# Chunk attention followed by a GELU MLP: plain V loads, tiles of the array by chunk parity, and a new order of transfers and products in the last five tiles

## The chip, the cores and the metric

The kernel runs on one NeuronCore of a Trainium2 chip. The metric is the device time of one execution in microseconds (us); lower is better. The core has five engines that run beside each other and meet at semaphores: TensorE (in the profile PE for matmuls, PEld for the loading of their weights), VectorE (DVE), ScalarE (ACT), GpSimd (POOL) and SyncE (SP), which issues nearly all DMAs of this kernel.

## The reference

```python
# q, k, v: 8 batches x 8 heads x 576 positions x 64, cut into 9 chunks of 64 positions
scores = matmul(q_c, k_c.T) / sqrt(64)               # each chunk attends to itself alone
attn = exp(scores - max) ; attn /= sum(attn) + 1e-9
x = matmul(attn, v_c)       # then heads side by side: 4608 tokens x 512
h = x @ w_in                # 512 x 2048
g = 0.5 * h * (1 + erf(h / sqrt(2)))
y = g @ w_out               # 2048 x 512, float32 out
```

## The kernel before

**Tiles.** The 4608 tokens are nine tiles of 512. Tiles 0 to 7 are the first eight chunks of each batch; tile 8 (`B`) gathers the ninth chunk of all batches. A tile's attention runs while the MLP of the tile before it runs: the outer loop has a step t for each MLP tile, and within step t stands the attention of tile n = t+1, the transposes of tile t+2, and loads of tiles t+2 and t+3. `FIRSTX` = 4 is the first tile whose attention takes the row form (`rows_av`, `rows_x`), which the change alters, and `FIRST7` = 3 is the first step whose second product has seven multiplications.

**The MLP of a step.** Both products are done with seven half-size products in the place of eight (Strassen's scheme in Winograd's form), so sums of blocks are needed as operands. `mm1_groups` makes h: 28 products of four matmuls, in the written order `FOUR` (steps 3 to 7). There `1a` is the first product of column group a, and `c1a`, `c2a`, `c3a` are copies of a bank by ACT, ACT and DVE. `6a` needs the third sum that `x_sums` (L602) makes of x. `c3c` (L706) writes into a buffer of the pool `ypool`. `h1` to `h3` call `h_sums` (L556, L557), two sums of h. Then `mm2_seven` makes y with seven products of 16 matmuls of 256 columns (L727, L736) in three PSUM banks X, Y and Z of a ring of three (`ps_mm`). Its fourth and fifth products need `h_third` (L561) and `h_fourth` (L565), sums of h by DVE. Before the change the order is: X; `rows_av`; Y; X again; Y again; Z = s3*T3 with its two output halves; Y += s4*w; Z += h*T4. `also(i)` marks the points where other work is inserted, as the lists `e2` say.

**The y buffers.** `ypool` has two buffers. A step from 3 to 7 takes three tiles of it in this order: one at `c3c`, y[0], y[1]. So `c3c` of the next step always takes the buffer of this step's y[0], and has to wait until both stores of y[0] have read it.

**Attention of a tile.** `quad_S` (L232) makes scores in four PSUM banks, 64 matmuls of 64 by 64 with the array cut into four tiles (row half r, column half o); ACT takes the exponential. V lies on 128 partitions as two chunks of 64 keys. `load_v_rows` (L120) puts the odd heads one chunk further than the even ones, so it takes nine DMAs for a tile, and 16 for tile 8. With that layout `rows_av` (L328) gives each of the four tiles of the array one matmul in each round of four: (0,0), (1,0), (1,1), (0,1). `rows_x` divides by the sums (L346, L348) and issues two DMA transposes (L340), the second when all is divided; they give the x of the next MLP. q and k are loaded (L108, L102; tile 8: L111, L106), cast by POOL (L154) and transposed by DMA (`flips_of`, L187). V is cast by POOL too (L206).

**Order.** The program is written out by hand (`manual_schedule`): each engine takes its own instructions in the order of the program, SP too. A DMA that waits on SP, or waits for its turn in the queue, holds back what is behind it. In step t before the change, SP has at the begin of `mm1_groups` (`ahead`): the transposes of q and k of tile t+2, and V of tile t+2 (steps 4, 5; in step 3 the q of tile 6); at `also(1)` the transposes of x, then q of tile t+3; then stores of y (L827) with k of tile t+3 at `also(4)`.

**The end.** Step 8 ends with `last_seven`: the last two products work on y[1], L811 adds its right half, L814 its left half, and `store_rows` (L821) stores a block of whole rows on two queues (SP and ACT).

Of the kernel before, what the change touches and what calls it, by code (L numbers as in the profile page):

```python
# [11 lines left out]
def kernel(  # L12
# [9 lines left out]
    nc = tc.nc  # L22
# [69 lines left out]
    def load_qk(t, nm, h0=0, h1=H):  # L92

        st = tiles[t]
        src = q if nm == "q" else k
        if nm + "f" not in st:
            st[nm + "f"] = stage_tile()[:].rearrange("p (h j d) -> p h j d", h=H, j=J)
            st[nm] = ld.tile([P, G, J, 2, D], bf16, tag=nm, name=f"{nm}_nat", bufs=1)
        raw = st[nm + "f"]
        if nm == "k" and t < B and t not in ORDERED:  # L100
            for n in range(CT // 2):
                nc.sync.dma_start(raw[:, :, n], src[t, :, P * n:P * (n + 1), :].rearrange("h key d -> key h d"))  # L102
        elif nm == "k" and t == B:
            for b in range(B):
                c, n = b % 2, b // 2
                nc.sync.dma_start(raw[CH * c:CH * (c + 1), :, n], src[b, :, MT:S, :].rearrange("h key d -> key h d"))  # L106
        elif t < B:
            nc.sync.dma_start(raw[:, h0:h1], src[t, h0:h1, 0:MT, :].rearrange("h (p j) d -> p h j d", j=J))  # L108
        else:
            for h in range(h0, h1):  # L110
                nc.sync.dma_start(raw[:, h], src[:, h, MT:S, :].rearrange("b (p j) d -> b p j d", j=J))  # L111

    def load_v_rows(t, parity=range(2)):

        if "vf" not in tiles[t]:
            tiles[t]["vf"] = stage_tile()[:].rearrange("p (h n d) -> p h n d", h=H, d=D)
        raw = tiles[t]["vf"]

        def go(to, rows):
            nc.sync.dma_start(to, rows.rearrange("h key d -> key h d"))  # L120
        last = CT // 2 - 1
        if t < B and 0 in parity:
            for n in range(CT // 2):
                go(raw[:, 0::2, n], v[t, 0::2, P * n:P * (n + 1), :])
        if t < B and 1 in parity:
            for n in range(last):
                go(raw[:, 1::2, n], v[t, 1::2, CH + P * n:CH + P * (n + 1), :])
            go(raw[0:CH, 1::2, last], v[t, 1::2, MT - CH:MT, :])
            go(raw[CH:P, 1::2, last], v[t, 1::2, 0:CH, :])
        if t == B:  # L130
            for b in range(B):
                for r in parity:
                    c, n = place(r, b)
                    go(raw[CH * c:CH * (c + 1), r::2, n], v[b, r::2, MT:S, :])

    def load_v_plain(t):
        tiles[t]["vf"] = stage_tile()[:].rearrange("p (h n d) -> p h n d", h=H, d=D)
# [84 lines left out]
    def quad_S(t, pairs=(0, 1)):  # L222

        st = tiles[t]
        if pairs[0] == 0:
            st["s_ps"] = four_banks("s_ps")
        s_ps = st["s_ps"]
        for g2, u, g, n, r, c, o, rs, os in quadrants():
            if g2 not in pairs:
                continue  # L230
            i = 2 * n + c
            nc.tensor.matmul(s_ps[g2][c][os, u, :].rearrange("p (j c) -> p j c", j=J),  # L232
                             st["kt"][rs, g * J + n, CH * c:CH * (c + 1)],
                             st["qt"][rs, g * J:(g + 1) * J, i * PC:(i + 1) * PC],
                             start=True, stop=True, tile_position=(CH * r, CH * o))
# [80 lines left out]
    def rows_av(t, last):  # L316
# [5 lines left out]
        for b in range(G * CT // 2):  # L322
            for c in range(2):
                for r in range(2):
                    bank, i = 2 * (b // NX) + r, b % NX
                    g, n, o = b // (CT // 2), b % (CT // 2), c ^ r
                    os, cs = slice(CH * o, CH * (o + 1)), slice(CH * c, CH * (c + 1))
                    nc.tensor.matmul(st["av"][bank][cs, i, :],  # L328
                                     st["pT", 2 * (g // 2) + c][os, CT // 2 * (g % 2) + n, :],
                                     st["v"][os, 2 * g + r, place(r, 2 * n + c)[1], :],  # L330
                                     start=True, stop=True, tile_position=(CH * o, CH * c))

    def rows_x(t):

# [404 lines left out]
    def halves(bank):  # L739
        return [bank[:, 0], bank[:, 1]]  # L740

    def mm2_seven(t, at={}):

        def also(i):
            for u in at.get(i, ()):
                u()
# [32 lines left out]
        TT(y[1][:, :, NH:], Z[:], s5[:], op=add)  # L779
        store(t, 1, 1, y)  # L780
        also(3)
        product(halves(Y), s[4], w[:, 1, :, 1], False)
        AC(y[0][:, :, NH:], Y[:])
        store(t, 0, 1, y)
        also(4)
        product(halves(Z), h[:, 1, :, 1], T[4], False)
        TT(y[1][:, :, :NH], Z[:], s2[:], op=add)
        store(t, 1, 0, y)
        also(5)

    def last_seven(t, h, w, s, T, banks, sums, y):
# [19 lines left out]
        product(Zs, s[3], T[3], True, lambda m: TT(y[1][:, m, NH:], Zs[m], s5[:, m], op=add))  # L811

        def row_block(m):
            TT(y[1][:, m, :NH], Zs[m], s2[:, m], op=add)  # L814
            store_rows(t, 1, m, y)
        product(Zs, h[:, 1, :, 1], T[4], False, row_block)

    def store_rows(t, th, m, y):
        for c in range(P // CH):
            m0 = ((th * (TH // P) + m) * (P // CH) + c) * S + MT  # L820
            (nc.sync if c == 0 else nc.scalar).dma_start(out[m0:m0 + CH, :], y[th][c * CH:(c + 1) * CH, m, :])  # L821

    def store(t, th, nh, y):

# [110 lines left out]
    with tc.manual_schedule():  # L935
# [126 lines left out]
        for t in range(1, NT):  # L1062
# [15 lines left out]
            elif t == 2:  # L1078
# [4 lines left out]
                def behind_k():  # L1083
# [1 line left out]
                    nc.gpsimd.tensor_copy(tiles[4]["q"][:, 0, 0, 0, 0:1], tiles[3]["kt"][:, G * J - 1, 0:1])  # L1085
                    pool_cast_qk(4)
                    flips_of(4)
                    load_v_rows(4)
                    load_qk(5, "q")
                    cast_v_rows(4, PO)  # L1090
                e1[f"i{G - 1}"] = [behind_k]
                e2 = one_tile(3, {8: [lambda: load_qk(5, "k")], 12: [lambda: quad_S(4, (0,))], 13: [lambda: quad_S(4, (1,)), lambda: act_table(Act.Gelu)]})
            elif n < NT:
                def ahead(t=t):
                    first = (0,) if t == B - 3 else ()
                    if FIRST7 < t < B - 2:
# [3 lines left out]
                    if FIRST7 < t < B - 2:  # L1100
                        load_v_rows(t + 2, [r for r in range(2) if r not in first])
                    if t == FIRST7:
                        load_ahead(t, "q")
                    if t == B - 1:
                        load_v_rows(B, (1,))
                        cast_v_rows(B, PO)
# [5 lines left out]
                def behind(t=t):  # L1112
                    load_ahead(t, "k")
# [12 lines left out]
                e2 = {1: [lambda: rows_av(n, tiles[n - 1]["Z"]), lambda: rows_x(n)], 2: [], 3: [], 4: [behind, lambda: x_sums(n)]}  # L1126
                if t == FIRST7:
                    e2[2] += [late_v]
                if FIRST7 < t < B - 2:
                    e2[1] += [lambda t=t: cast_v_rows(t + 2, PO)]  # L1130
                if t == B - 2:
                    e2[1] += [lambda: load_v_rows(B, (0,))]
                if t + 3 < NT:
                    if t > FIRST7:
                        e2[1] += [lambda t=t: load_ahead(t, "q")]
                    if t + 3 < B:
                        e2[1] += [lambda t=t: pool_cast_q(t + 3)]
                if n + 1 < NT:
                    e2[1] = [lambda: act_table(Act.Exp)] + e2[1]
                    e2[2 if t == FIRST7 else (2, 0)] = e2[2] + [lambda: quad_S(n + 1), lambda: act_table(Act.Gelu)]  # L1140
            phase(t, e1, e2, between=last_rows if t == 1 else {})
# [1 line left out]
_INS = ['q', 'k', 'v', 'moe_w_in', 'moe_w_out']  # L1143
# [26 lines left out]
```

## Time and profile before

| | |
|---|---|
| time, median of 3 runs | 272.56 us (271.09 to 273.3) |
| profiled execution, first to last instruction | 273.1 us; no other time of it is given, and it lies within the range of the three runs |
| PE busy | 262.1 us, 96% |
| DVE, ACT, POOL busy | 73%, 68%, 29% |
| granted clock of TensorE | 0.997 on average |
| DMA | 56.60 MB, mean 207 GB/s; the queue of SP takes 79.2% of the 16 engines' span |

How to read it: a busy time of PE is from the start of a matmul to its modelled end, and matmuls overlap, so that starts tell more than ends. In the lists of instructions in order of time the columns are: start in us from the span's start, duration of the merged group, engine (a q behind it: its sequencer, which issues DMAs), line, operation, output<-inputs, shapes, count, and in brackets the idle time before it with what ended it.

### The profile page before, as it was taken

Reading aid. Unit: us, or ns where it says so; the run is one execution under the profiler, and the core shown is the slowest. Engines: PE = TensorE matmul, PEld = TensorE weight load, DVE = VectorE, ACT = ScalarE, POOL = GpSimd, SP = SyncE. Lnnn points to the kernel's source line nnn. Section 1 sums busy time; section 2 is a strip of 40 time slices with the busy share of each in tenths; the row PEclk is TensorE's granted clock in tenths of the full one; section 3 lists DMA queues with packets and bytes.
Section 4 is the critical chain, followed back from the end, with each engine's and each line's share of the span. In section 5 each row is a group of like instructions: output and inputs, shape, how many; then the busy total and the mean of one; then the engine's idle time right before and its main releaser. Section 6 shows DMA issues by size and latency. Waiting matters only on the chain. (4 is left out here: it accounts for less than half of the span.)

```text
span 273.1 us, 7571 instructions
## 1 busy us (share of the span) xinstructions
PE 262.1 (96%) x3080; PEld 194.2 (71%) x3080; DVE 198.1 (73%) x363; ACT 186.9 (68%) x363; POOL 79.3 (29%) x127
## 2 busy tenths in 40 slices
PE   8989999999999999999989999989998999999993
PEld 3454453486458544888878888878887888888782
DVE  2663787959898697599479937995699559946851
ACT  3557756788767967886679669956995699338600
POOL 2734667351370240342333043311062011000000
PEclk9999999999999999999999999999999999999998
DMA  6999999997979799898989989998895571340005
GB/s 201 261 344 406 395 396 232 265 278 162 337 206 223 198 204 207 242 258 149 275 218 252 193 167 307 238 188 144 252 228 113 107 217 32 74 159 2 1 4 154
DMA packets 128564, 56.60 MB, mean 207 GB/s; under 512 B 103952, under 2 KB 123408, under 8 KB 128528
## 3 DMA queue, kind: packets, MB, share of 16 engines
q1 hardware_dynamic: 128208, 55.59, 79.2%
q8 instruction: 24, 0.39, 0.6%
q10 hardware_dynamic: 320, 0.52, 0.5%
q14 instruction: 12, 0.10, 0.1%
HBM read 36.70 MB, written 9.44 MB: 169 GB/s over the span
## 5 line engine op out<-in xcount | busy, mean ns | idle before, releaser
L658 PEld LDWEIGHTS <-w_in_s 128*128 128x128 bf16 x464 | 45.2, 98 | 7.4 <-DVE x_t L602 1.1
L658 PEld LDWEIGHTS <-w_in_sb 128*128 128x128 bf16 x348 | 33.9, 98 | 7.2 <-issue 1.0
L206 POOL CAST v_nat<-arrival 128x1024 bf16<-128x1024 f32 x14 | 16.3, 1164 | 61.8 <-DMA arrival<-in_v_dram 54.8
L727 PEld LDWEIGHTS <-h_s 128*128 128x128 bf16 x304 | 29.3, 98 | 5.6 <-DVE h_s L561 2.1
L836 PE MATMUL y_ps<-w_out_sb,h 128*128 128x512 bf16 x144 | 33.0, 380 | 0.0
L658 PE MATMUL h_Y<-x_t,w_in_s 128*128 128x256 bf16 x232 | 32.0, 272 | 1.0 <-DVE x_t L602 0.8
L658 PE MATMUL h_X<-x,w_in_sb 128*128 128x256 bf16 x232 | 32.6, 273 | 0.0
L727 PEld LDWEIGHTS <-h 128*128 128x128 bf16 x288 | 28.2, 98 | 3.5
L154 POOL CAST k_nat<-arrival 128x512 bf16<-128x512 f32 x34 | 22.3, 692 | 25.3 <-DMA arrival<-in_k_dram 20.8
L154 POOL CAST q_nat<-arrival 128x512 bf16<-128x512 f32 x33 | 19.6, 633 | 26.1 <-DMA arrival<-in_q_dram 25.9
L727 PE MATMUL y_ps<-w_t,h_s 128*128 128x256 bf16 x208 | 25.1, 273 | 1.6 <-DVE h_s L561 1.6
L836 PEld LDWEIGHTS <-h 128*128 128x128 bf16 x144 | 13.4, 98 | 15.0 <-issue 0.2
L693 ACT COPY h_Y<-h_X 128x512 f32<-128x512 f32 x29 | 16.4, 582 | 9.7 <-PE h_X L658 9.5
L727 PE MATMUL y_ps<-w_out_sb,h 128*128 128x256 bf16 x192 | 22.9, 273 | 0.0
L933 ACT ACT_TABLE_LOAD x16 | 20.5, 1283 | 1.0 <-PEq L1154 0.7
L665 ACT ACTIVATE h<-h_Y 128x512 bf16<-128x512 f32 x29 | 17.0, 593 | 1.8 <-PE h_Y L658 1.3
L665 ACT ACTIVATE h<-h_X 128x512 bf16<-128x512 f32 x29 | 17.2, 598 | 1.4 <-PE h_X L658 0.8
L239 ACT ACTIVATE pT<-s_ps 128x512 bf16<-128x512 f32 x28 | 14.5, 601 | 4.3 <-PE s_ps L232 4.2
L658 PE MATMUL h_Z<-x_t,w_in_s 128*128 128x256 bf16 x116 | 17.4, 273 | 0.0
L658 PE MATMUL h_Z<-x_t,w_in_sb 128*128 128x256 bf16 x116 | 16.9, 272 | 0.4 <-DVE h_d L709 0.4
L658 PE MATMUL h_Y<-x,w_in_s 128*128 128x256 bf16 x116 | 16.9, 273 | 0.0
L706 DVE COPY h_a<-h_Y 128x512 f32<-128x512 f32 x8 | 5.5, 691 | 14.8 <-PE h_Y L658 14.8
(148 smaller groups left out, 490.9 us busy)
## 6 DMA issues: line engine op xcount, KB each, us to landing
out_dram<-y_sb SPq DMA_DIRECT2D x32, 256.0 KB
arrival<-in_q_dram SPq DMA_DIRECT2D x7, 1024.0 KB
arrival<-in_k_dram SPq DMA_DIRECT2D x24, 256.0 KB
arrival<-in_v_dram SPq DMA_DIRECT2D x42, 128.0 KB
arrival<-in_moe_w_out_dram SPq DMA_DIRECT2D x4, 1024.0 KB
arrival<-in_v_dram SPq DMA_DIRECT2D x8, 256.0 KB
arrival<-in_moe_w_in_dram SPq DMA_DIRECT2D x4, 512.0 KB
arrival<-in_moe_w_in_dram SPq DMA_DIRECT2D x2, 1024.0 KB
```

What stands on the lines that cost most here:

```text
L154: copy(st[nm][:, g].rearrange("p j r d -> p r j d"), st[nm + "f"][:, 2 * g:2 * g + 2])
L206: copy(st["v"][:, r::2, :, :D], st["vf"][:, r::2])
L239: nc.scalar.activation(pT[:].rearrange("p u (c j) -> p u c j", j=J), s_ps[g2][c][:].rearrange("p u (j c) -> p u c j", j=J), Act.Exp, scale ...
L658: nc.tensor.matmul(banks[g + name][:, i], lhs[:, kk, i], rhs[:, kk], start=fresh and i == kk == 0, stop=(kk == 1), skip_group_check=True)
L665: nc.scalar.activation(h[:, j:j + 2, m], src[:], Act.Gelu)
L693: AC(banks[g + "Y"][:], banks[g + "X"][:])
L706: (AC if i == 0 else DV)(sums[g, i][:], banks[g + "Y"][:])
L727: nc.tensor.matmul(out[m], lhs[:, f, m * P:(m + 1) * P], rhs[:, f, :], start=fresh and f == 0 and (m == 0 or len(out) == 3), stop=(f == FH ...
L836: nc.tensor.matmul(y_ps[:], st["h"][:, f, ms * P:(ms + 1) * P], w_out_sb[:, f, :], start=(f == 0), stop=(f == FF - 1))
L933: nc.scalar.activation(act_scratch[:], rest[:, 0:1], func)
```

## The change

Five edits, all from tile 4 on (or step 3 on):

1. **V in four plain transfers.** `load_v_plain` brings V of tiles 4 to 7 in four DMAs of 256 KB with all heads alike (tile 8: eight DMAs). `place` is plain for these tiles.
2. **Scores and AV by chunk parity.** In `quad_S` the scores of chunk parity c go to the partitions of column half c, and the bank is chosen by r. `rows_av` then uses the tiles (0,0), (0,0), (1,1), (1,1) in each round of four: two tiles of the array, each twice in a row, where there were four.
3. **Order of the transfers.** V of tile t+2 and q of tile t+3 leave the begin of the step and `also(1)`. q and k of tile t+3 are issued at `also(2)`, behind the transposes of x. V of tile t+2 is issued at `also(4)` in steps 3 and 4, and at `also(2)` ahead of q and k in steps 5 and 6. V is cast at the begin of the next step (tiles 5, 6) or right behind its load (tiles 7, 8).
4. **Ninth q.** Its eight DMAs name the position within the chunk first and the batch second, (p b) where it was (b p). The scores of tile 8 read it with a step of eight elements.
5. **Late sums of h later, and the stores.** `mm2_seven` makes Z = h*T4 first, adds it to s2 on DVE, then W = s3*T3 in a fourth turn of the ring, which DVE adds twice into y[1]; y[1] is stored by one DMA of 512 KB. The product with s4, and with it the last store of y[0], is now last. In `last_seven` each half of the columns of y[1] is stored as soon as it is there.

```diff
-                nc.sync.dma_start(raw[:, h], src[:, h, MT:S, :].rearrange("b (p j) d -> b p j d", j=J))
+                nc.sync.dma_start(raw[:, h], src[:, h, MT:S, :].rearrange("b (p j) d -> p b (j d)", j=J))
...
-    def place(r, i):
+    def place(r, i, t=0):
+        if t >= FIRSTX:
+            return i % 2, i // 2
...
-            nc.tensor.matmul(s_ps[g2][c][os, u, :].rearrange("p (j c) -> p j c", j=J),
+            if t >= FIRSTX:
+                o, os = c, slice(CH * c, CH * (c + 1))
+            nc.tensor.matmul(s_ps[g2][r if t >= FIRSTX else c][os, u, :].rearrange("p (j c) -> p j c", j=J),
                              st["kt"][rs, g * J + n, CH * c:CH * (c + 1)],
+                             st["qt"][rs, g * J:(g + 1) * J, i:P:CT] if t == B else
...
-                                     st["pT", 2 * (g // 2) + c][os, CT // 2 * (g % 2) + n, :],
-                                     st["v"][os, 2 * g + r, place(r, 2 * n + c)[1], :],
-                                     start=True, stop=True, tile_position=(CH * o, CH * c))
+                                     st["pT", 2 * (g // 2) + r][cs, CT // 2 * (g % 2) + n, :],
+                                     st["v"][cs, 2 * g + r, n, :],
+                                     start=True, stop=True, tile_position=(CH * c, CH * c))
...
-        product(halves(Z), s[3], T[3], True, lambda m: also((2, m)))
-        TT(y[1][:, :, NH:], Z[:], s5[:], op=add)
-        store(t, 1, 1, y)
+        product(halves(Z), h[:, 1, :, 1], T[4], True, lambda m: also((2, m)))
+        TT(s2[:], Z[:], s2[:], op=add)
         also(3)
+        W = bank_mm()
+        product(halves(W), s[3], T[3], True)
+        TT(y[1][:, :, NH:], W[:], s5[:], op=add)
+        TT(y[1][:, :, :NH], W[:], s2[:], op=add)
+        store_whole(t, 1, y)
+        also(4)
         product(halves(Y), s[4], w[:, 1, :, 1], False)
         AC(y[0][:, :, NH:], Y[:])
         store(t, 0, 1, y)
-        also(4)
-        product(halves(Z), h[:, 1, :, 1], T[4], False)
-        TT(y[1][:, :, :NH], Z[:], s2[:], op=add)
-        store(t, 1, 0, y)
...
+        def row_block(m, nh):
+            cols = slice(nh * NH, (nh + 1) * NH)
+            TT(y[1][:, m, cols], Zs[m], (s2, s5)[nh][:, m], op=add)
+            store_rows(t, 1, m, y, cols)
+        product(Zs, s[3], T[3], True, lambda m: row_block(m, 1))
+        product(Zs, h[:, 1, :, 1], T[4], False, lambda m: row_block(m, 0))
...
-                    load_v_rows(4)
+                    load_v_plain(4)
...
                 def ahead(t=t):
-                    first = (0,) if t == B - 3 else ()
-                    if FIRST7 < t < B - 2:
-                        load_v_rows(t + 2, first)
                     if t + 2 < NT:
                         flips_of(t + 2)
...
+                    if t in (FIRST7 + 1, FIRST7 + 2):
+                        cast_v_rows(t + 1, PO)
+
+                def qk(t=t):
+                    if t + 3 < NT:
                         load_ahead(t, "q")
+                        if t + 3 < B:
+                            pool_cast_q(t + 3)
+                        load_ahead(t, "k")
                 def late_v(t=t):
-                    load_v_rows(t + 2)
-                    cast_v_rows(t + 2, PO)
+                    if t + 2 < NT:
+                        load_v_plain(t + 2)
+                    if t >= FIRST7 + 2 and t + 2 < NT:
+                        cast_v_rows(t + 2, PO)
...
+                e2[2 if t > FIRST7 + 1 else 4].append(late_v)
+                e2[2].append(qk)
```

More of the change, by code (lines that the diff above doesn't have):

```diff
@@ L129, in load_v_rows, with load_v_plain @@
             go(raw[CH:P, 1::2, last], v[t, 1::2, 0:CH, :])
+    def load_v_plain(t):
+        tiles[t]["vf"] = stage_tile()[:].rearrange("p (h n d) -> p h n d", h=H, d=D)
         if t == B:
             for b in range(B):
[L132 to L137, printed above, removed]
+                c, n = b % 2, b // 2
+                nc.sync.dma_start(tiles[t]["vf"][CH * c:CH * (c + 1), :, n], v[b, :, MT:S, :].rearrange("h key d -> key h d"))
+            return
         for n in range(CT // 2):
@@ L325, in rows_av @@
                     bank, i = 2 * (b // NX) + r, b % NX
[L326 to L327 removed]
+                    g, n = b // (CT // 2), b % (CT // 2)
+                    cs = slice(CH * c, CH * (c + 1))
                     nc.tensor.matmul(st["av"][bank][cs, i, :],
[L329 to L331 removed]
+                                     st["pT", 2 * (g // 2) + r][cs, CT // 2 * (g % 2) + n, :],
+                                     st["v"][cs, 2 * g + r, n, :],
+                                     start=True, stop=True, tile_position=(CH * c, CH * c))
     def rows_x(t):
@@ L810, in last_seven, with store_rows, store_whole @@
             store_rows(t, 0, m, y)
[L811 to L818, printed above, removed]
+        def row_block(m, nh):
[4 more added lines that the diff above has]
+        product(Zs, h[:, 1, :, 1], T[4], False, lambda m: row_block(m, 0))
+    def store_rows(t, th, m, y, cols=slice(0, d_model)):
         for c in range(P // CH):
             m0 = ((th * (TH // P) + m) * (P // CH) + c) * S + MT
-            (nc.sync if c == 0 else nc.scalar).dma_start(out[m0:m0 + CH, :], y[th][c * CH:(c + 1) * CH, m, :])
+            (nc.sync if c == 0 else nc.scalar).dma_start(out[m0:m0 + CH, cols], y[th][c * CH:(c + 1) * CH, m, cols])
+    def store_whole(t, th, y):
+        m0 = t * S + th * TH
+        nc.sync.dma_start(out[m0:m0 + TH, :].rearrange("(m p) n -> p m n", p=P), y[th][:])
     def store(t, th, nh, y):
@@ L1125 @@
                     pool_cast_q(t + 2)
[L1126 to L1137, printed above, removed]
+                e2 = {1: [lambda: rows_av(n, tiles[n - 1]["Z"]), lambda: rows_x(n)], 2: [], 3: [], 4: [lambda: x_sums(n)]}
+                e2[2 if t > FIRST7 + 1 else 4].append(late_v)
+                e2[2].append(qk)
                 if n + 1 < NT:
                     e2[1] = [lambda: act_table(Act.Exp)] + e2[1]
-                    e2[2 if t == FIRST7 else (2, 0)] = e2[2] + [lambda: quad_S(n + 1), lambda: act_table(Act.Gelu)]
+                    e2.setdefault(2 if t == FIRST7 else (2, 0), []).extend([lambda: quad_S(n + 1), lambda: act_table(Act.Gelu)])
             phase(t, e1, e2, between=last_rows if t == 1 else {})
```

8 lines of the change are left out of this document (removed).

## The prediction

> **What bounds the kernel now.** I read the page first, then the table of windows cut at the steps, then PE in order of time wherever a step was longer than its matmuls.
>
> ```profile
> span 273.1 us, 7571 instructions
> PE 262.1 (96%) x3080; PEld 194.2 (71%) x3080; DVE 198.1 (73%) x363; ACT 186.9 (68%) x363; POOL 79.3 (29%) x127
> ...
> 135.95:163.22 27.27, 26.41 (x355) 23.00 (x353) 19.83 (x39) 20.63 (x37) 7.63 (x11) 1.00 0.96 206
> 163.22:190.30 27.08, 26.39 (x355) 23.01 (x353) 21.42 (x42) 20.63 (x37) 6.98 (x11) 1.00 1.02 220
> ...
> 165.00:170.00 5.00, 5.00 (x48) 4.41 (x46) 3.29 (x6) 4.60 (x9) 2.17 (x4) 1.00 1.07 329
> ```
>
> The window rows give length, busy time of PE, PEld, DVE, ACT and POOL, clock, DMA share and GB/s; the first two are steps 4 and 5. PE bounds the kernel, at full clock. The DMA engines are almost as full (0.96, 1.02), so what stands early in their queue delays what stands late. All that PE can gain in the middle of the kernel is its few stalls:
>
> ```profile
> 121.20 0.60 PE L658 MATMUL h_Z<-x_t,w_in_sb 128*128 128x256 bf16 x4 [0.36 <-DVE h_d L709]
> ...
> 135.95 1.47 PE L658 MATMUL h_X<-x,w_in_sb 128*128 128x256 bf16 x12
> 138.27 0.61 PE L658 MATMUL h_Y<-x_t,w_in_s 128*128 128x256 bf16 x4 [0.84 <-DVE x_t L602]
> ...
> 173.32 0.60 PE L658 MATMUL h_Y<-x,w_in_s 128*128 128x256 bf16 x4
> 173.76 0.60 PE L658 MATMUL h_Z<-x_t,w_in_sb 128*128 128x256 bf16 x4
> ...
> 181.79 1.80 PE L727 MATMUL y_ps<-w_t,h_s 128*128 128x256 bf16 x15
> 184.25 1.05 PE L727 MATMUL y_ps<-w_t,h_s 128*128 128x256 bf16 x8 [0.67 <-DVE h_s L561]
> ...
> 209.24 1.47 PE L727 MATMUL y_ps<-w_t,h_s 128*128 128x256 bf16 x12
> 211.63 1.05 PE L727 MATMUL y_ps<-w_t,h_s 128*128 128x256 bf16 x8 [0.91 <-DVE h_s L561]
> ```
>
> Four matmuls of 256 columns take 0.437 us from start to start (173.32 to 173.76), so 0.109 each. Counted from starts, the stalls are 1.01 us at 138.27 (2.32 less 12 x 0.109), 0.82 at 184.25 (2.46 less 15 x 0.109) and 1.08 at 211.63; at 121.20 I use the 0.36 of the row.
>
> **The change part by part.** E is the end of a step.
>
> *AV on two tiles of the array.*
>
> ```profile
> 151.17 0.65 PE L328 MATMUL av_ps<-v_nat,pT 64*64 64x65 bf16 x56
> ...
> 151.72 0.21 PE L328 MATMUL y_ps<-v_nat,pT 64*64 64x65 bf16 x1
> 151.95 1.91 PE L736 MATMUL y_ps<-w_t,h_s 128*128 128x256 bf16 x16
> ...
> 158.16 0.74 PE L232 MATMUL s_ps<-q_t,k_t 64*64 64x64 bf16 x64
> ...
> L328 PEld LDWEIGHTS <-pT 64*64 64x64 bf16 x320 | 3.3, 106 | 1.1 <-issue 0.8 <-DVE h_s L557 0.2
> ```
>
> Today 64 matmuls start within 0.55 us (151.17 to 151.72): 16 rounds of four at 0.034 us, in which each tile has one matmul. 65 columns at 0.109/256 need 0.028, so a round is about one streaming time of a tile, and the weights of the next matmul hide behind it. With two tiles, each twice in a row, a round takes two such times: 16 x 0.034 more and a few ns of issue in each, +0.6 us a tile, +3.0 for tiles 4 to 8. Lower end: 32 matmuls of 0.028 are 0.89, so +0.34 each, 1.7 in all. Upper end: weights of a tile that is busy are not hidden, 0.106 for each of two matmuls in 16 rounds, 3.4 us, +2.8 each. I take 3.0, because today's round shows a tile receiving new weights every 0.034 us.
>
> *Scores.* Each round still uses all four tiles once, and neighbours of the kind (0,0), (1,0) stand in today's AV: 0. Tile 8 reads q with a step of eight elements, which no row shows. Between nothing and a doubling of 0.74 (the row at 158.16) I take +0.3. The Trainium skill (SBUF — State Buffer, Door 1: The DMA port swizzle) says that SBUF wants two hits in each 16-byte line for full bandwidth; eight bf16 elements are just one line, so by it every column would pay. No run here shows that yet; the sum would stay within the +0.74 of my upper end.
>
> *Late sums.*
>
> ```profile
> 182.98 1.22 DVE L561 TENSOR_TENSOR h_s<-h 128x2048 bf16<-128x2048 bf16 x1
> 187.05 0.69 DVE L779 TENSOR_TENSOR y_sb<-y_ps,y 128x512 f32<-128x512 f32 x1 [1.72 <-PE y_ps L727]
> 189.15 0.76 DVE L602 TENSOR_TENSOR x_t<-x 128x512 bf16<-128x512 bf16 x2 [1.40 <-DMA x<-x_r]
> 189.82 0.88 DVE L602 TENSOR_TENSOR x_t<-x,x_t 128x512 bf16<-128x512 bf16 x2
> ```
>
> s3 (L561) is done at 184.20 and would be wanted only one product and the scores after 183.4, some 2.4 us later: the stalls of 0.82 and 1.08 go, -1.9. Next late are `x_sums`, now behind the two additions of W. W ends one product (1.75) before E, the additions start about 0.3 later and take 0.69 each, so the sums start at about E-0.1. Three take 0.34 each from start to start (189.15 to 189.82 for two) and the third ends at E+1.0. `6a` wants it after twelve matmuls, at E+1.31: no stall, 0.3 in hand; if that cover goes, each 0.1 more costs 0.1. The added addition costs nothing, since DVE waits 1.72 us ahead of L779. `c1a` gets Y's bank, behind ACT's copy of the last product: +0.05 at four steps, +0.2.
>
> *Transposes of x ahead of q.*
>
> ```profile
> 127.30 0.57 SPq L108 DMA_DIRECT2D arrival<-in_q_dram  x1
> 127.96 5.47 SPq L340 DMA_TRANSPOSE x<-x_r  x2
> ...
> 137.12 0.76 DVE L602 TENSOR_TENSOR x_t<-x 128x512 bf16<-128x512 bf16 x2 [3.69 <-DMA x<-x_r]
> ...
> 158.19 2.69 SPq L340 DMA_TRANSPOSE x<-x_r  x2
> 160.93 0.58 SPq L108 DMA_DIRECT2D arrival<-in_q_dram  x1
> 161.60 2.06 SPq L827 DMA_DIRECT2D out_dram<-y_sb  x3
> 163.71 7.11 SPq L102 DMA_DIRECT2D arrival<-in_k_dram  x4
> ...
> 185.97 5.67 SPq L111 DMA_DIRECT2D arrival<-in_q_dram  x8
> ```
>
> In step 3 the q of 1024 KB stood ahead of the transposes, which took 5.47 us of SP and not 2.69, and let DVE wait 3.69. With q behind them this goes: -1.01 at 138.27. The stall at 121.20 has another cause:
>
> ```profile
> 115.61 2.48 POOL L154 CAST q_nat<-arrival 128x512 bf16<-128x512 f32 x4 [2.95 <-DMA arrival<-in_q_dram]
> 116.73 0.88 DVE L556 TENSOR_TENSOR h_s<-h 128x512 bf16<-128x512 bf16 x1
> ...
> 170.74 0.42 DVE L556 TENSOR_TENSOR h_s<-h 128x512 bf16<-128x512 bf16 x1
> 171.53 0.68 DVE L706 COPY h_sb<-h_Y 128x512 f32<-128x512 f32 x1
> 173.99 2.29 POOL L154 CAST k_nat<-arrival 128x512 bf16<-128x512 f32 x4 [3.87 <-DMA arrival<-in_k_dram]
> ```
>
> A sum of h beside casts by POOL took 0.88 us, alone 0.42. V of tile 4 in four DMAs brings this q earlier; between 0 and -0.36 I take -0.2.
>
> *The last store of y[0].* This decides the sign. `c3c` (L706, `h_sb`) takes y[0]'s buffer and waits for its stores. It comes 8.3 us into a step (171.53 less 163.22), and product `3c`, 10.1 us into it (173.32), needs it. Today the last store of y[0] is issued ahead of k (161.60, 163.71) and lands in time, so no row shows the wait. Now it is issued last, and in steps 3 and 4 it stands behind q, k, y[1] and V. DVE has divided at E-7.4 (182.98 against 190.30); the second transpose then takes SP about 1.3. So from E-6 the queue gets stores of 256, 512 and 256 KB and three loads of 1024 KB: 4096 KB. Slow end: q, three stores and k, 2816 KB, took from 160.93 to the cast of k at 173.99; less some 2 us from issue to landing (the transposes of x, issued by 160.88, let `x_sums` start at about 163), that is 11.1 us, and 4096 KB take 16.1: landing at E+12. Fast end: the 329 GB/s of the window from 165: 12.7 us, landing at E+8.7. `c3c` adds 0.8, so PE stalls for 0 to 2.7 us. I take the middle, E+10.5: 1.2. In step 5 SP itself sets the time: from E-5.4 four V, eight q (5.67) and eight k at the same 0.6 to 0.7 reach the store at E+8 to E+9, landing about E+10.5 again. Steps 4, 5 and 6 meet it: +3.6, between 0 and 8. Step 6 loads only V, so step 7 is free of it.
>
> *What else stands behind.* V of tiles 5 and 6 lands before that store, by E+11; its casts take no longer than the 2.29 of k, and AV comes 15.2 us into a step (151.17 less 135.95): 0, but one for one if V is over a microsecond later. The transposes of q and k stand behind the store and have until the scores, 22 us into the step: 0. The ninth q is needed a step later: 0.
>
> *The end.*
>
> ```profile
> 265.76 3.66 SPq L821 DMA_DIRECT2D out_dram<-y_sb  x4
> 268.50 0.42 DVE L814 TENSOR_TENSOR y_sb<-y_ps,y 128x256 f32<-128x256 f32 x1 [0.45 <-PE y_ps L727]
> ```
>
> From the last addition (268.92) to the end are 4.2 us, in which two DMAs of 128 KB go out; half of these bytes is now sent before. -0.6, between 0 and -1.
>
> **Sum.** Added: 3.0 + 0.3 + 0.2 + 3.6 = 7.1. Gone: 1.9 + 1.01 + 0.2 + 0.6 = 3.7. The profiled execution of 273.1 becomes 276.5; it lies 0.5 above the median of 272.56, so the forecast is 276.0, with 273.5 to 278.5 as this case's own range.
>
> **The rivals.**
>
> *The stores land in time: not slower.* If the queue runs at the fast pace, `c3c` finds its buffer free and the 3.6 fall away: 272.4. The point is a landing at E+9.3. For it speaks that 329 GB/s occur at all; against it that steps 4 and 5 average 206 and 220.
>
> *The array takes the next matmul of the same tile at today's pace, and the stores land in time*: 3.0 less again, 269.4. Against it: a round equals a tile's streaming time.
>
> *Weights are not hidden* on a tile used twice in a row: half of the way to the upper end, +1.4 at each of five tiles, 283.0.
>
> *POOL blocks DVE at `x_sums`.* q of tile t+3 lands near E+1 (1280 KB at the slow pace from E-6, and 2). Were it a microsecond earlier, each sum could wait for a cast (0.57) and the third would end 1.0 later, 0.7 too late, at four steps: 278.8. The rows at 116.73 and 170.74 show the effect; the landing behind the sums speaks against. The Trainium skill (SBUF — State Buffer, Who interferes with whom) says that a `tensor_tensor` with both inputs in SBUF and a GpSimd instruction that reads SBUF exclude each other for a whole instruction. By that rule this happens wherever they meet, and the trace agrees: 0.88 for 0.42.
>
> **How the numbers follow.** Forecast 0.45, stores in time 0.25, both free 0.14, weights not hidden 0.09, POOL 0.07. One per cent, 2.7 us, is about what a measurement of this kernel can tell from no change. Of the forecast's 0.45 some 0.12 lie below 275.3, and 0.01 of the second case below 269.8. So faster 0.15, within 1% 0.37, slower 0.48. The range leaves out the lower half of "both free" and most of "weights not hidden": 269.0 to 281.0.
>
> **What would show it.** AV of a tile: 1.4 us from its first start to the next L736, against 0.78. `h_sb` (L706) in steps 4, 5 and 6 with idle time ahead of it, ended by a DMA of y, and PE waiting for it 10 us into the step. No stall at L727 for L561, none for `x_t` at 2 us into step 4. Less than 4 us from the last L814 to the end. The forecast is wrong if `h_sb` finds no wait, or if AV stays at 0.8 or goes beyond 2 us.

## The result and the profile after

The changed kernel takes 281.32 us (median of 6 runs, 280.92 to 281.64), the kernel before 272.05 (6 runs, 270.66 to 274.03). The ratio is 1.0324, 95% interval 1.0284 to 1.0363: 3.2% slower. Ratios, here and below, are formed from undisturbed executions alone. The forecast was 276.0 with a range of 269.0 to 281.0, so the sign was the one called likeliest and the size was outside.

The profiled execution of the changed kernel has a span of 279.4 us and a time of 281.34, so 1.9 us lie outside the span. The first lines of its page, and two rows of the 40 slices:

```profile
span 279.4 us, 7535 instructions
PE 266.5 (95%) x3080; PEld 198.2 (71%) x3080; DVE 199.9 (72%) x368; ACT 186.9 (67%) x363; POOL 77.2 (28%) x127
...
PE   7889999999999999999999999999589999999994
...
PEclk9999999999999999999999999999959999999999
```

PE is about as full as before but for slices 29 and 30, and in slice 30 TensorE is granted half its clock. The next fence is the table of windows of the changed kernel, cut at steps 3 to 7 (columns as in the prediction):

```profile
108.53:135.43 26.90, 26.77 (x354) 23.43 (x352) 20.07 (x37) 20.25 (x37) 7.05 (x10) 1.00 0.87 215
135.43:162.06 26.63, 26.63 (x354) 23.44 (x352) 20.13 (x40) 20.67 (x37) 6.79 (x11) 1.00 0.97 209
162.06:189.28 27.22, 26.95 (x355) 23.55 (x353) 21.38 (x40) 20.78 (x37) 7.81 (x12) 1.00 0.94 214
189.28:223.96 34.68, 30.35 (x354) 25.66 (x352) 20.15 (x40) 20.77 (x37) 6.97 (x12) 0.90 0.71 168
223.96:249.81 25.85, 25.85 (x290) 22.90 (x288) 20.11 (x40) 15.63 (x29) 2.02 (x2) 1.00 0.27 74
```

Four of the five steps are within 0.7 us of those of the profile before (27.0, 27.3, 27.1, 27.5, 25.5). Step 6 alone has 34.68 in the place of 27.5. In order of time, PE there, then DVE, then SP's DMA issues:

```profile
198.98 0.60 PE L663 MATMUL h_Z<-x_t,w_in_s 128*128 128x256 bf16 x4
203.91 1.01 PE L663 MATMUL h_Y<-x,w_in_s 128*128 128x256 bf16 x4 [4.33 <-DVE h_sb L711]
204.72 1.06 PE L663 MATMUL h_Z<-x_t,w_in_sb 128*128 128x256 bf16 x4
205.57 1.06 PE L663 MATMUL h_Y<-x,w_in_s 128*128 128x256 bf16 x4
```

```profile
197.27 0.42 DVE L562 TENSOR_TENSOR h_s<-h_s,h 128x512 bf16<-128x512 bf16 x1
203.17 0.69 DVE L711 COPY h_sb<-h_Y 128x512 f32<-128x512 f32 x1 [5.47 <-DMA out_dram<-y_sb]
```

```profile
184.05 4.22 SPq L139 DMA_DIRECT2D arrival<-in_v_dram  x4
188.32 5.33 SPq L111 DMA_DIRECT2D arrival<-in_q_dram  x8
193.69 5.70 SPq L106 DMA_DIRECT2D arrival<-in_k_dram  x8
199.49 0.57 SPq L832 DMA_DIRECT2D out_dram<-y_sb  x1
200.16 0.41 SPq L838 DMA_DIRECT2D out_dram<-y_sb  x1
```

The wait that the prediction was looking for is there: `c3c` (L711, `h_sb`) stands behind a DMA of y, and PE behind `c3c`. From starts, PE lost 203.91 less 198.98 less 4 x 0.109, 4.49 us. But it comes once, not three times, and it is three to four times as long as forecast. It has a sequel: four matmuls then take 0.85 from start to start (204.72 to 205.57) and not 0.44. The windows of the stall, of the stretch behind it and of the rest of the step:

```profile
199.40:203.90 4.50, 0.18 (x2) 0.01 (x1) 0.69 (x1) 0.07 (x1) 2.78 (x6) 0.78 1.15 275
203.90:208.75 4.85, 4.84 (x23) 3.34 (x23) 3.81 (x6) 3.12 (x6) 0.66 (x2) 0.50 0.88 193
208.75:223.96 15.21, 15.21 (x239) 13.36 (x237) 9.72 (x22) 8.10 (x14) 0.00 (x0) 1.00 0.47 104
```

For the 4.85 us behind the stall the granted clock is 0.50. The 23 matmuls in them cost 0.105 each on top, 2.4 us. The stall and its sequel are 6.9 us together. The clock fell within the stall: if it has just the two values 1.00 and 0.50, a mean of 0.78 over 4.50 us is half clock for the last 2.0 of them, so it fell at about 201.9, some 2.5 us after PE had run dry (199.4), and stayed low for 6.8 us.

Which store is it? SP issued four DMAs of V, eight of q and eight of k before the store of y[1] (L832, the whole tile in one DMA) at 199.49, and the last store of y[0] (L838) at 200.16. The list of DMAs issued from 196 to 206 gives their size and the time from issue to landing:

```profile
out_dram<-y_sb SPq DMA_DIRECT2D x1, 512.0 KB, 3.6
out_dram<-y_sb SPq DMA_DIRECT2D x1, 256.0 KB, 4.4
```

The 512 KB of y[1] landed at 203.1, and `c3c` began at 203.17; the 256 KB of y[0] landed at 204.6, 1.4 us after `c3c` had begun. So the wait is for y[1]. Step 4 agrees:

```profile
142.74 0.80 SPq L838 DMA_DIRECT2D out_dram<-y_sb  x1
```

```profile
143.77 0.68 DVE L711 COPY h_sb<-h_Y 128x512 f32<-128x512 f32 x1
```

`c3c` begins 1.0 us after the last store of y[0] was issued; the page's median from issue to landing of these stores is 3.5. So `c3c` does not wait for y[0]. The reading that fits these rows is that the pool hands out the buffer that was given back first in the order of the program: before the change that would be y[0]'s, though no row of that kernel shows a wait; with the store of y[0] last it is y[1]'s. In steps 3 and 4 the store of y[1] stands ahead of V, and lands in time. In step 5 it stands behind all twenty loads, and in step 6 behind V of tile 8, with nothing else in the queue.

The other differences: AV of a tile, and the scores of tile 8, in the changed kernel (PE in order of time):

```profile
123.03 1.11 PE L333 MATMUL av_ps<-v_nat,pT 64*64 64x65 bf16 x58
...
124.16 1.92 PE L741 MATMUL y_ps<-w_t,h_s 128*128 128x256 bf16 x16
...
176.53 1.43 PE L333 MATMUL av_ps<-v_nat,pT 64*64 64x65 bf16 x57
...
178.01 1.92 PE L741 MATMUL y_ps<-w_t,h_s 128*128 128x256 bf16 x16
...
184.23 0.74 PE L236 MATMUL s_ps<-q_t,k_t 64*64 64x64 bf16 x64
...
217.62 2.03 PE L236 MATMUL s_ps<-q_t,k_t 64*64 64x64 bf16 x64
```

AV takes 1.13 from its first start to the next product (0.78 before); in step 5 it takes 1.48. The scores of tile 8 take 2.03, those of tile 7 0.74. The stalls at L561 and at 2 us into step 4 are gone; L561 and L565 are L566 and L570 here, and no row of PE waits for them.

### The profile page after: what moved, and what is told of

Read it like the earlier page. It is cut to its first block, busy times and chain, and to the rows that moved or that the text cites. A ratio compares the mean times of both kernels' runs of the same rounds, so it can differ in the third digit from the quotient of the medians.

```text
span 279.4 us, 7535 instructions
## 1 busy us (share of the span) xinstructions
PE 266.5 (95%) x3080; PEld 198.2 (71%) x3080; DVE 199.9 (72%) x368; ACT 186.9 (67%) x363; POOL 77.2 (28%) x127
## 4 chain that ended last, share of the span: by engine, by line
PE 74%; DMA 8%; SPq 6%; DVE 5%; ACT 3%; POOL 2%; issue 1%; DVEq 0%; ACTq 0%; POOLq 0%
PE y_ps L732 20%; PE h_Y L663 12%; PE y_ps L847 11%; PE h_Z L663 8%; PE h_X L663 7%; PE h_ps L528 4%; DMA arrival<-in_moe_w_out_dram 4%; PE y_ps L741 3%; PE h_ps L685 2%; DMA arrival<-in_k_dram 2%; SPq L106 2%; PE s_ps L236 2%; SPq L111 2%; PE av_ps L333 2%; SPq L139 1%
## 5 line engine op out<-in xcount | busy, mean ns | idle before, releaser
L208 POOL CAST v_nat<-arrival 128x1024 bf16<-128x1024 f32 x14 | 15.5, 1128 | 60.1 <-DMA arrival<-in_v_dram 60.0
L156 POOL CAST k_nat<-arrival 128x512 bf16<-128x512 f32 x34 | 21.2, 659 | 19.6 <-DMA arrival<-in_k_dram 16.7
L663 PE MATMUL h_Y<-x,w_in_s 128*128 128x256 bf16 x116 | 18.2, 287 | 4.3 <-DVE h_sb L711 4.3
L663 PE MATMUL h_Z<-x_t,w_in_sb 128*128 128x256 bf16 x116 | 17.8, 282 | 0.1
L711 DVE COPY h_a<-h_Y 128x512 f32<-128x512 f32 x8 | 5.5, 691 | 15.4 <-PE h_Y L663 15.4
```

What stands on the lines that cost most here:

```text
L156: copy(st[nm][:, g].rearrange("p j r d -> p r j d"), st[nm + "f"][:, 2 * g:2 * g + 2])
L208: copy(st["v"][:, r::2, :, :D], st["vf"][:, r::2])
L663: nc.tensor.matmul(banks[g + name][:, i], lhs[:, kk, i], rhs[:, kk], start=fresh and i == kk == 0, stop=(kk == 1), skip_group_check=True)
```

## The experiments

Times of the kernel before spread over almost 8 us within a set of runs (270.92 to 278.72 in 25 runs), those of the changed kernel over 0.7. The median of the kernel before also differs from set to set: 272.05, 274.33, 272.20, 274.94 and 273.16. So a kernel is compared by its ratio to the runs of the kernel before in its own set, and single steps are read from the profiles.

**The kernel before again (e0_before).**

> The kernel before once more, unchanged. The changed kernel's time lies 1.9 us above its profiled span (281.34 against 279.4). If the same holds for the kernel before, its median of 272.05 belongs to a span of about 270.1, and the profiled execution of 273.1 that the prediction was worked out from was a late one of some 275. Then a profile of a usual execution shows a span of 269 to 271 and has lost stalls worth about 3 us: the first to look at are those at 121.20, 138.27, 184.25 and 211.63. The rival, that the profiled execution was a usual one, expects a span near 273 with the same four stalls, and a time outside the span near zero.

The ratio to itself is 0.9958 (0.9882 to 1.0034). The profiled execution took 274.08 with a span of 272.3: 1.8 us lie outside. So the execution that the prediction was worked out from took an estimated 274.9 (273.1 and 1.8), and not 272.56. Two of its four stalls are not in this profile, those of `x_t` (1.01) and at 121.20 (0.36); the other two are:

```profile
183.55 1.05 PE L727 MATMUL y_ps<-w_t,h_s 128*128 128x256 bf16 x8 [0.92 <-DVE h_s L561]
...
210.91 1.05 PE L727 MATMUL y_ps<-w_t,h_s 128*128 128x256 bf16 x8 [0.92 <-DVE h_s L561]
```

The span was not between 269 and 271 as expected: 274.08 is a usual time in this set, whose median for the kernel before is 274.33. That some 1.8 us lie outside the span holds. Which of the four stalls a usual execution has can't be told from two profiles.

**A buffer of its own for `c3c` of step 6 (e1_own_buffer).**

```diff
-                    pair = ypool.tile([P, 4, TH], f32, tag="y", name="h_sb")
+                    pair = (stage_tile()[:, :4 * TH].rearrange("p (a e) -> p a e", a=4) if t == B - 2 else
+                            ypool.tile([P, 4, TH], f32, tag="y", name="h_sb"))
```

> The changed kernel, with the order of all transfers as it is; only c3c of step 6 writes into a stage buffer instead of a buffer of ypool, so that it waits for no store. Theory A: the stall of 4.4 us at 203.9 is c3c waiting for the store of y[1] (the pool hands out the buffer that was given back first, and that is now y[1]'s), and the half clock that follows (some 23 matmul pairs at 0.105 more each, 2.4 us) is its consequence. Then step 6 falls from 34.7 to about 27.9, the clock stays at full speed, and the time is 281.3 less 6.8: 274.5. Rival B: the transfers of step 5 are too many in any order, and with this wait gone the next one (transposes of q and k of tile 8, x) stalls PE about as long: 278 or more.

Measured 274.69, ratio 1.0059 (1.0013 to 1.0105). The windows of steps 5 and 6:

```profile
162.29:189.65 27.36, 26.88 (x355) 23.56 (x352) 21.54 (x40) 20.73 (x37) 7.91 (x12) 1.00 0.92 214
189.65:217.57 27.92, 27.92 (x354) 24.56 (x352) 21.45 (x40) 20.68 (x37) 8.10 (x12) 1.00 0.86 202
```

Step 6 takes 27.92 and PE is busy through all of it, at full clock. Not one transfer was moved, so the transfers of step 5 as such stall nothing: the wait for one buffer did. Rival B is out.

**The ninth q and k behind the store of y[1] (e2_qk_behind).**

```diff
-                e2[2].append(qk)
+                e2[4 if t + 3 == B else 2].append(qk)
```

> The changed kernel with the sixteen loads of the ninth q and k in step 5 moved from also(2) to also(4), behind the store of y[1]; the last store of y[0] stays behind them. Theory A (c3c waits for y[1]'s store): y[1] is issued behind four DMAs of V instead of twenty, lands about 3 us into step 6, the stall and the half clock go: 274.5. The prediction's own reading (c3c waits for y[0]'s last store): that store is still behind sixteen loads, issued about 11 us into step 6, and the stall of over 4 us stays: 280 to 282.

Measured 274.71, ratio 1.0103 (1.0058 to 1.0148). SP and DVE in order of time:

```profile
190.37 0.38 SPq L832 DMA_DIRECT2D out_dram<-y_sb  x1
190.80 5.38 SPq L111 DMA_DIRECT2D arrival<-in_q_dram  x8
196.22 5.61 SPq L106 DMA_DIRECT2D arrival<-in_k_dram  x8
201.92 0.57 SPq L838 DMA_DIRECT2D out_dram<-y_sb  x1
```

```profile
198.54 0.42 DVE L562 TENSOR_TENSOR h_s<-h_s,h 128x512 bf16<-128x512 bf16 x1
198.88 0.68 DVE L711 COPY h_sb<-h_Y 128x512 f32<-128x512 f32 x1
```

`c3c` runs without a wait 3 us before the last store of y[0] is even issued. The prediction's reading, that it waits for y[0], is refuted; theory A holds.

**AV with its tiles in turn (e3_av_alternate).**

```diff
-            for c in range(2):
-                for r in range(2):
+            for r in range(2):
+                for c in range(2):
```

> The changed kernel with the two inner loops of AV exchanged: the tiles of the array in a round are (0,0), (1,1), (0,0), (1,1) where they were (0,0), (0,0), (1,1), (1,1). A tile's AV took 1.13 us from its first start to the next product, 0.78 in the kernel before. If the cost is that the same tile follows itself at once and its weights are not hidden, AV goes back to about 0.8, and the time falls by 0.35 at five tiles: 279.6. If it is only that two tiles stream where four did (32 matmuls of 0.028 are 0.89), nothing changes: 1.1 and 281.3. The second is likelier.

Measured 280.83, ratio 1.0257 (1.0152 to 1.0362), and the row of AV is unchanged:

```profile
123.72 1.11 PE L333 MATMUL av_ps<-v_nat,pT 64*64 64x65 bf16 x58
...
124.86 1.38 PE L741 MATMUL y_ps<-w_t,h_s 128*128 128x256 bf16 x11
```

1.14 for 1.13. That a tile is used twice in a row costs nothing; what is left as the cause is that there are two tiles for 64 matmuls. The stall of step 6 is still in this kernel: the row of `c3c`'s product has a wait of 5.2 us, and the half clock follows.

**The ninth q as before (e5_own_buffer_q9_old, e12_own_buffer_q9_old_again)**, on top of the kernel with its own buffer for `c3c`.

```diff
-  ... src[:, h, MT:S, :].rearrange("b (p j) d -> p b (j d)", j=J))
+  ... src[:, h, MT:S, :].rearrange("b (p j) d -> b p j d", j=J))
...
-                             st["qt"][rs, g * J:(g + 1) * J, i:P:CT] if t == B else
```

> The kernel of e1_own_buffer with the ninth q loaded and read as before (batch first, the scores of tile 8 read runs of 16 elements). In the changed kernel the scores of tile 8 took 2.03 us and those of tiles 4 to 7 0.74. Theory: the step of eight elements in the moving operand costs the 1.29; then tile 8 takes 0.74 and the time falls from e1's 274.7 to 273.4, so that its ratio to the kernel before goes from 1.006 to about 1.001. Rival: it is the new placing of the scores on the array together with tile 8's q; then 2.0 stays and so does 1.006.

Measured 272.54, ratio 1.0012 (0.9974 to 1.0049), and the scores of tile 8:

```profile
210.66 0.74 PE L236 MATMUL s_ps<-q_t,k_t 64*64 64x64 bf16 x64
```

The placing on the array is the new one, and 0.74 is back: the step of eight elements costs the 1.29. The ratio fell as expected, though the intervals of the two overlap. A repetition gave 273.28 and 1.0038 (1.0001 to 1.0075). It was expected 1.8 above e11_order_old_v, and came out 4.1 below it, for the reason given there:

> The kernel of e5_own_buffer_q9_old once more, for a comparison on the same chip: ratio to the kernel before 1.00 as in e5 (1.0012), and 1.8 above e11_order_old_v if AV is all that tells the two apart.

Its PE names what AV of tile 6 waits for, once the first matmul is out:

```profile
177.43 0.21 PE L332 MATMUL av_ps<-v_nat,pT 64*64 64x65 bf16 x1
178.04 1.08 PE L332 MATMUL av_ps<-v_nat,pT 64*64 64x65 bf16 x56 [0.40 <-POOL v_nat L208]
```

**The new products and stores alone (e6_before_late_sums)**, in the kernel before (`mm2_seven`, `last_seven`, `store_whole` as in the diff of the change, nothing else).

> The kernel before with the new order of the products and stores alone (mm2_seven, last_seven, the store of y[1] in one DMA); V, AV, scores, the ninth q and the order of the loads stay as before. Theory: the two stalls of 1.08 at L561 go, and the end is shorter by 0.4 to 0.5; c3c takes y[1]'s buffer, whose store is here issued ahead of k and so lands in time: 2.6 us faster than the kernel before, ratio 0.990. Rival, by which late sums of h are paid back elsewhere (a wait of c3c, x_sums behind the two additions): ratio 0.997 to 1.01, with a new stall in steps 4 to 7.

Measured 272.06, ratio 1.0008 (0.9980 to 1.0037). That misses the 0.990 and lies in the rival's range. The windows of steps 5 and 6 show the gain, and the row of the last stores where most of it goes:

```profile
161.29:187.54 26.25, 26.23 (x354) 23.04 (x352) 20.94 (x40) 20.67 (x37) 7.36 (x11) 1.00 0.99 216
187.54:214.12 26.58, 26.35 (x355) 23.03 (x353) 21.09 (x40) 20.77 (x37) 6.09 (x10) 1.00 0.73 181
```

```profile
L823 ACTq DMA_DIRECT2D out_dram<-y_sb x6: 552/589/2326, 262.6 to 267.7; - x6
```

Steps 5 and 6 are 1.9 us shorter than in the other profile of the kernel before (27.32 and 27.37). But the longest of ACT's six DMA issues (shortest, median and longest in ns) took 2.33 us; it is the first of them, and from the last addition to the end it is 5.4 us, not 4.1.

**The same with the q of tile 6 behind the transposes of x (e7_late_sums_q_behind).**

> e6_before_late_sums, and the q of tile 6 in step 3 issued behind the transposes of x, as in the other steps. The profiled execution of the prediction lost 1.01 us there, that of e0_before nothing. Theory: the wait is there in some executions alone; then the median is 0 to 0.5 us below e6 and the spread of the times smaller. Rival: it is there in most; 1.0 below e6.

Measured 273.29, ratio 1.0041 (1.0013 to 1.0068): neither. In its profile PE waits 1.3 us for `x_t` one step later (in step 5). The profile of e6 has a wait for `x_t` at neither place, so the two profiles don't tell whether the move of the load caused this one or whether it is one of the waits that some executions have.

**The same with the old end, and the same again (e9_late_sums_old_end, e10_late_sums_again).**

> e6_before_late_sums with the end (last_seven, store_rows) as in the kernel before: only the order of products and stores of steps 3 to 7 is new. In the profile of e6 the two stalls at L561 were gone (steps 5 and 6 took 26.25 and 26.58, in e0_before 27.32 and 27.37), but from the last addition to the end it took 5.4 us (4.1 in e0_before), because the first store that ACT issued took 2.33 us where it takes 0.57 in the others. Theory: e6 loses most of its gain there in most executions; then this kernel shows a store of 0.57 and is 1.8 to 2.2 faster than the kernel before, ratio 0.992 to 0.994. Rival: that store was an accident of one execution, and the gain goes elsewhere, in stalls that vary from execution to execution: ratio 0.997 to 1.004, as e6.

> The kernel of e6_before_late_sums once more, for a second profile and more times. Theory of a lasting loss at the end: the first store that ACT issues takes over 2 us again, and the ratio is 1.00 again. Rival: it takes 0.57, the span is below 270, and the ratio lies between 0.990 and 1.00 with the spread of single executions.

Measured 1.0002 (0.9949 to 1.0055) and 1.0046 (0.9994 to 1.0098). The slow DMA issue is no accident of one execution: 2.46 and 2.38 us, again the first one of ACT, also with the old end. In the one profile with the old end, of that kernel's slowest execution, it seems to cost little (4.35 from the last addition to the end), and the ratio is still 1.000. In the second of the two profiles step 6 took 28.05, with three stalls behind DVE at `c3c` and its additions, and `c3c` itself waited 1.70 us for a DMA of y: the store of y[1], which there stands behind the eight loads of q. So the wait for y[1] comes with the new order of the stores alone, before any load is moved. The two stalls at L561 go, as all profiles with this order show, and the time does not fall: in e6 and e10 some 1.6 us are lost at the end (5.4 from the last addition, where e7, with the same end, takes 3.7), and the rest in waits that differ from execution to execution. Which of them the usual execution has stays open.

**V in plain transfers and the two tiles alone (e8_before_two_tiles)**, in the kernel before (edits 1 and 2).

> The kernel before with V in plain transfers and scores and AV by chunk parity alone (edits 1 and 2); q, products, stores and the places of the loads stay as before. Theory: AV takes 1.13 instead of 0.78 at five tiles, so 1.8 us slower, ratio 1.006 to 1.007. Rival: five V transfers fewer in a step make room in SP and in the DMA queue, and the stalls at L561 or at x_t shrink: ratio 1.000 or below.

Measured 273.91, ratio 1.0064 (1.0035 to 1.0093): 1.7 us slower, the 1.8 of AV at five tiles. Its five runs lie within 0.4 us (273.86 to 274.27), where the kernel before beside it had 270.62 to 275.35. In its profile one of the two stalls at L561 is left (0.8 us) and none for `x_t`; so the room of which the rival speaks may be there in part, but the time doesn't show it.

**The new order with V as before (e11_order_old_v).** V in nine transfers, scores and AV on four tiles, as in the kernel before; all else as in the kernel of the ninth q as before.

> The kernel of e5_own_buffer_q9_old with V loaded in nine transfers a tile and scores and AV on four tiles of the array, as in the kernel before: what is left of the change is the new order of transfers, products and stores, with the buffer of its own for c3c in step 6. Theory: AV goes back from 1.13 to 0.78 at five tiles; 1.8 below e12_own_buffer_q9_old_again, and, with the two stalls at L561 gone and the end 0.5 shorter, 1.5 to 2.5 below the kernel before: ratio 0.991 to 0.995. Rival: nine transfers in place of four hold the store of y[1], the transposes and the casts of V back, and new stalls (V for AV, x_t) take the gain: ratio 0.997 to 1.005.

Measured 277.39, ratio 1.0185 (1.0123 to 1.0246). Windows of steps 4 to 7, then SP and DVE in order of time:

```profile
135.49:161.78 26.29, 26.27 (x354) 23.10 (x352) 20.37 (x40) 20.73 (x37) 7.32 (x11) 1.00 0.93 210
161.78:188.08 26.30, 26.28 (x354) 23.07 (x352) 20.71 (x40) 20.72 (x37) 7.48 (x12) 1.00 0.99 215
188.08:215.67 27.59, 26.31 (x355) 23.10 (x352) 20.82 (x40) 20.67 (x37) 7.17 (x12) 1.00 0.85 196
215.67:243.99 28.32, 25.89 (x290) 22.52 (x288) 20.08 (x40) 15.72 (x29) 2.08 (x2) 1.00 0.34 87
```

```profile
212.04 10.86 SPq L120 DMA_DIRECT2D arrival<-in_v_dram  x16
223.01 0.55 SPq L828 DMA_DIRECT2D out_dram<-y_sb  x1
```

```profile
227.09 0.69 DVE L707 COPY h_sb<-h_Y 128x512 f32<-128x512 f32 x1 [2.93 <-DMA out_dram<-y_sb]
```

Steps 4 and 5 have no stall left. Then the same mechanism strikes a step later, where `c3c` has no buffer of its own: V of tile 8 is now sixteen DMAs, the store of y[1] is issued 7.3 us into step 7, and PE loses 2.0 us there. A further 1.4 are lost in step 6 by late transposes of k, and ACT's first store took 2.33 us again. AV did go back to four tiles, and both the theory and the rival were wrong on the size: the rival's mechanism, at the store of y[1], cost more than AV gave.

## Why the prediction failed in its size

- **The last store of y[0], +3.6 forecast: wrong step.** "`c3c` (L706, `h_sb`) takes y[0]'s buffer" was read from the order of allocation before the change. The new order of the stores also changes which buffer comes back first. The last store of y[0] landed 11.3, 13.2 and 15.3 us into the next step (issued at 142.74, 171.39 and 200.16, landing 4.0, 3.9 and 4.4 later), where 10.5 was taken, and nothing waited for it; the twenty DMAs of step 5 were counted, but for the wrong store. Measured: a wait for y[1]'s store of 4.5 us in one step, 2.4 of half clock behind it, 6.9 together. That this lies within the bounds of 0 to 8 is luck, since they were worked out for three waits for the other store and without the half clock. The sign is partly luck too: with this one wait taken away the ratios are 1.0059 (e1) and 1.0103 (e2), about the 1% that the prediction counted as no change.
- **The half clock** was not in the sum at all. A stall of 4.5 us was followed by it, the one of 2.0 in the last experiment was not (its windows show 1.00). The Trainium skill (TensorE: Matmul & The Clock Gate, Part 1) has the clock halve after some 3.4 us of idleness and recover after as long a busy stretch. The trace differs in both: the clock fell some 2.5 us after PE had run dry, and 4.85 us of matmuls passed until it was back.
- **AV, +3.0 forecast: 2.1.** 0.35 at four tiles, almost the lower bound of 0.34, and 0.70 at one. The starts of the 64 matmuls take 1.01 us and not 0.55, which is the doubling of the rounds as forecast less 0.1; but the pause from the last of them to the next product shrank from 0.23 to 0.13, and that was not in the term. The other 0.35, at tile 6, is V: POOL's two casts of it ended at 176.8 (begun at 174.33, 2.49 together), after AV had begun (176.53). The 0 that the prediction took for a late V was wrong there.
- **Scores, +0.3 forecast: 1.29**, above the upper bound of 0.74. A doubling was no bound; the row became 2.7 times as long. The Trainium skill (SBUF — State Buffer, Door 1: The DMA port swizzle) has every element pay at this step; the runs agree, and the cost is larger than the prediction allowed it.
- **Late sums, -1.9: right in the profile**, and every profile with the new order has lost the two stalls. The net gain in time isn't shown by the runs of this edit alone.
- **Transposes ahead of q, -1.0 and -0.2: right for the profiled execution** (the changed kernel has neither stall; the one at 121.20 is 0.5 by its starts, not the 0.36 of its row). Whether it is a gain over a usual execution is open, since the second profile of the kernel before has neither.
- **The end, -0.6: 0.5.** From the last addition, 275.64, to the end, 279.36, it is 3.7, where it was 4.2. `c1a` and its 0.2 left no trace.
- **POOL beside DVE**: not at `x_sums`. In step 5 two sums of h ran beside the casts of k (0.62 and 0.71 us, in step 4 0.41 and 0.42), `c3c` came 0.5 later into the step, and PE has a gap of 0.3 at 173.82, 0.2 more than at the same place of step 4. That the one brings about the other is argued, not shown. The sums beside the casts of V (0.86 and 1.41 for 0.69) show no product waiting behind them.
- **The base.** Terms as measured: 2.1 for AV, 1.3 for the scores and 6.9 for the stall with its half clock, less 1.9 for the late sums, 1.0 and 0.5 for the stalls at 138.27 and 121.20, and 0.5 for the end, are 6.4 (6.6 with the 0.2 of step 5). The two profiled spans differ by 6.3, where 3.4 were forecast. The other 2.4 of the miss of 5.3 are the conversion: the prediction subtracted 0.5 to come from the span to the median, where 1.9 are to be added to a span for a time. The profiled execution of the kernel before, an estimated 274.9, lay 2.9 above the median of 272.05.

The rivals: with the wait taken away, as the stores in time would have it, the time is 274.7 (ratio 1.0059) and not 272.4. The array at the old pace, and weights that are not hidden, are both out: AV costs 0.35, whatever the order of the tiles. Two of the prediction's sums don't come out: half of the way from the 0.6 in its sum to the upper end of 2.8 is 1.1 a tile, so that weights not hidden would be 281.5 and not 283.0; and its chances add up to 0.36 within 1% and 0.49 slower, not 0.37 and 0.48.

No kernel tried beats the kernel before; three are level with it (1.0002, 1.0008 and 1.0012, each with an interval that holds 1), and the repetitions of the last two gave 1.0046 and 1.0038.

## What to carry to other kernels

When a store is moved, look up again which buffer the next tile gets: a pool that hands out the one given back first changes its order with the stores, and then every DMA ahead of that store is in the way of the next step. Ask of a long wait of TensorE what follows it: here one of 4.5 us cost 2.4 more in half clock, and one of 2.0 us left the clock at 1.00. Where the limit lies was not measured. Before a span of one profiled execution is compared with a median, find what lies outside the span and how far the executions spread.

## What was not expected of the hardware

Two tiles of the array took 64 matmuls of 65 columns in 1.13 us, four tiles in 0.78, and the order of the tiles made no difference (1.14). A moving operand read with a step of 16 bytes took 2.03 us for 64 matmuls of 64 columns on four tiles, a contiguous one 0.74. In four profiles the first DMA that ACT issues at the end took 2.33 to 2.46 us (e6, e9, e10, e11), in the others none took more than 0.87. The four have the new order of products with V in nine transfers in common, but so has e7, where it took 0.57; the cause stays open.
